# Chunk 0 of a delta-rule layer: Y from 128-row products, joint 16-blocks, and an earlier place for the second inversion

## The chip, the cores and the metric

The kernel runs on one NeuronCore of a Trainium2 chip. The metric is the device time of one execution in microseconds (us), as the median of several runs. TensorE (PE) multiplies, its weight loads (PEld) overlap with it, and VectorE (DVE), ScalarE (ACT) and GpSimd (POOL) work beside it. SyncE (SP) issues most DMAs. Each engine takes its instructions strictly in its own order and waits on semaphores of the others.

## What is computed

```python
k_n = k / (norm(k, axis=-1) + 1e-6)              # batch 4, heads 8, seq 768, head_dim 48
state = zeros(B, H, 48, 48)
for t in range(768):
    y[t] = q[t] @ state
    v_old = state^T k_n[t]
    state = state + beta[t] * outer(k_n[t], v[t] - v_old)
x = y as (3072 tokens, 384)                      # 384 = 8 heads x 48
h = x @ w_in                                     # 384 -> 2048
out = softplus(h) @ w_out                        # 2048 -> 384
```

All inputs and outputs are fp32.

## The kernel before

The sequence is cut into 12 chunks of 64 steps. In a chunk the recurrence is a triangular system: the 64x64 Gram matrix of the keys is inverted below its diagonal, and then U = T V, Y = P U and the new state follow as products. Two chunks share one inversion (`invert(u)`, u = 0 for chunks 0 and 1, u = 1 for chunks 2 and 3, ...). It works on 32x32 diagonal blocks that are spread over partitions, a row at a time, in pairs of instructions: a product into `tmp` (L294) and a sum into `Z` (L299). For u = 0 the blocks are 16x16 and two of them are done side by side, each with instructions of its own, on DVE; for later u one 32x32 block is done on POOL. Before the loop stand `norms(u)` (L222 to L242), a mask on POOL (L261) and two products on DVE (L271, L275).

The 16-blocks of chunk pair 0 are then put together by `join(s)`: a first product on PE (L324), its copy on ACT (L326), a second product on PE (L331), a subtraction and a transpose on DVE (L332, L333). `cross_a` and `cross_b` (L343) make 64x64 inverses of the 32x32 ones. `u_all` (L445) makes U, `y_all` (L476) makes Y, `state` (L457) the state.

The expert layer runs over 7 passes of 1, 1, 2, 2, ... chunks. A block of it is `hidden(i, g)` (L577, six fp32 products with 256 columns in the first pass), three ACT instructions (L582 to L584: abs, exp, ln), `softplus` on DVE (L595), and one step later `output` (L623). The weights come as 64-bit words. `feed` writes one word on an engine and starts a load, `top` makes the high halves (two casts on ACT, L525) into one of the two buffers `ex`, and `convert` puts them together on DVE (two instructions, L535) and so frees that buffer. `hidden(0, g)` needs the converted weights f = 2g and 2g + 1.

Nothing is scheduled by a planner up to the first block: the order is that in which the program is written, on every engine. Afterwards `plan` hangs steps at blocks: what stands at t is issued behind `hidden` of block t, what stands at t + 0.5 behind its `softplus` and its weight steps.

`y_all(0)` needs the layer's input as 3 tiles of 128 rows, each made of two heads' 48 rows and two 16-row pieces of a fourth pair's heads. The products have 64 rows per head, so the 16-row pieces are moved by six DMAs from x4 to x (L495), three issued by SP and three by ACT. `warm` (L684) issues products whose result nobody reads.

Of the kernel before, what the change touches and what calls it, by code (L numbers as in the profile page):

```python
# [21 lines left out]
P = 128  # L22
# [12 lines left out]
PULL0 = 8000  # L35
# [25 lines left out]
def deltanet_moe(ctx, tc, kT, qT, kI, vN, beta, wts, out, outT):  # L61
# [58 lines left out]
    GRAM_COPIES, OFFS = ((nc.scalar.copy, nc.scalar.copy),) * 2, {}  # L120

# [30 lines left out]
    tmp = const.tile([P, 2 * n_tmp], F32, name="tmp")  # L152

# [65 lines left out]
    def norms(u, lq):  # L219
# [21 lines left out]
        nc.vector.tensor_scalar(ncT, cT, -1.0, None, op0=ALU.mult)  # L241
        nc.vector.transpose(nn, nt)  # L242
        for j in range(2):
            NN[2 * u + j] = nn[:, j * NP:(j + 1) * NP]
        yield 900
        return cT, ncT

    def invert(u):
# [10 lines left out]
        for a in blocks:  # L259
            d = (slice(None), slice(a, a + n), slice(a, a + n))  # L260
            nc.gpsimd.affine_select(  # L261
                out=lq[d], in_=lq[d],
                compare_op=ALU.is_gt, fill=0.0, base=0, pattern=[[1, n], [-1, n]],
                channel_multiplier=0)
# [4 lines left out]
        for a in blocks:  # L269
            d = (slice(None), slice(a, a + n), slice(a, a + n))  # L270
            nc.vector.tensor_tensor(lq[d], lq[d],  # L271
                                    ncT[:, a:a + n].unsqueeze(1).to_broadcast([P, n, n]),
                                    op=ALU.mult)
            yield 200 + n * n
            nc.vector.tensor_tensor(Z[d], lq[d],  # L275
                                    cT[:, a:a + n].unsqueeze(2).to_broadcast([P, n, n]),
                                    op=ALU.mult)
            yield 200 + n * n
        if u < N16:

            parts = one.tile([P, 2, NP, HB + QB], F32, name=f"x{u + 1}")
            for j in range(2):
                ld = LDS[2 * u + j] = parts[:, j, :, 0:HB]
                LDS[2 * u + j, 1] = parts[:, j, :, HB:]
                nc.gpsimd.memset(ld[:, :, QB:], 0.0)
                nc.scalar.activation(ld[:, :, 0:QB], LTD[u][:, j * NP:(j + 1) * NP, 0:QB],
                                     AF.Copy, scale=half)
        engine.tensor_copy(Z.rearrange("p a b -> p (a b)")[:, 0:HB * HB:HB + 1], cT)
        for j in range(n - 2, 0, -1):
            r = n - 1 - j  # L290
            t = [tmp[:, k * n_tmp:k * n_tmp + r * j].rearrange("p (r j) -> p r j", j=j)
                 for k in range(len(blocks))]
            for a, o in zip(blocks, t):
                engine.tensor_tensor(  # L294
                    o, Z[:, a + j + 1:a + n, a + j:a + j + 1].to_broadcast([P, r, j]),
                    lq[:, a + j:a + j + 1, a:a + j].to_broadcast([P, r, j]), op=ALU.mult)
            for a, o in zip(blocks, t):
                z = Z[:, a + j + 1:a + n, a:a + j]
                engine.tensor_tensor(z, z, o, op=ALU.add)  # L299
            yield cost * 2 * len(blocks) * (160 + r * j)  # L300
# [4 lines left out]
    def turn_back(u):  # L305
        nc.vector.transpose(TT[u][:, :, HB:].rearrange("p q c -> p c q"),
                            Z.rearrange("p c j -> p j c"))
# [120 lines left out]
    def p_half(s, g):  # L428
        pt = hid([P, 8, C])
        for i in range(8):  # L430
            for ab in range(2):
                nc.tensor.matmul(pt[tk[ab], i, :], kts[s][dr[ab], 8 * g + i, :],
                                 bv[dr[ab], ab, 8 * g + i, 0:C], start=True, stop=True)
        return pt

    def mask_p(g, ab, pt):
        gs = slice(8 * g, 8 * g + 8)
        nc.vector.tensor_tensor(
            bv[tk[ab], ab, gs, 0:C], pt[tk[ab]],
# [561 lines left out]
```

## Time and profile before

| | us |
|---|---|
| median of 3 runs | 570.24 |
| lowest and highest | 569.12, 572.97 |
| span of the profiled execution | 568.9 |

Of the span PE is busy 543.8 us (96%), PEld 447.6 (79%), DVE 372.8 (66%), ACT 362.2 (64%), POOL 196.4 (35%). The mean granted TensorE clock is 0.979. The chain of work that ended last is 75% PE, 9% DVE, 7% POOL, 3% ACT, 2% DMA. The instruction stream of PE itself comes by DMA too: queue 8, kind "instruction", 60 packets, 0.98 MB. The rest is read from timelines: each row gives a start, a duration, the engine, the line of the kernel, the operation with its tiles and shapes, how many instructions were merged, and in brackets the idle time ahead of it with what ended it.

### The profile page before, as it was taken

Reading aid. Unit: us, or ns where it says so; the run is one execution under the profiler, and the core shown is the slowest. Engines: PE = TensorE matmul, PEld = TensorE weight load, DVE = VectorE, ACT = ScalarE, POOL = GpSimd, SP = SyncE. Lnnn points to the kernel's source line nnn. Section 1 sums busy time; section 2 is a strip of 40 time slices with the busy share of each in tenths; the row PEclk is TensorE's granted clock in tenths of the full one; section 3 lists DMA queues with packets and bytes.
Section 4 is the critical chain, followed back from the end, with each engine's and each line's share of the span. In section 5 each row is a group of like instructions: output and inputs, shape, how many; then the busy total and the mean of one; then the engine's idle time right before and its main releaser. Section 6 shows DMA issues by size and latency. Waiting matters only on the chain.

```text
span 568.9 us, 18018 instructions
## 1 busy us (share of the span) xinstructions
PE 543.8 (96%) x7683; PEld 447.6 (79%) x7683; DVE 372.8 (66%) x721; ACT 362.2 (64%) x702; POOL 196.4 (35%) x338
## 2 busy tenths in 40 slices
PE   4678998999999999999999999999999999999997
PEld 4456776789997888887888888888888888888885
DVE  5968785999947777548947477947375647343434
ACT  4525869898857983745873756863657855455353
POOL 4301898007982048810688000797000000000000
PEclk9857999999999999999999999999999999999999
DMA  9666862313340123220123220021220020010001
GB/s 202 169 221 206 222 208 73 72 58 72 86 99 3 31 50 79 54 69 36 31 55 73 57 71 30 3 65 35 70 86 3 1 51 22 15 57 0 1 1 55
DMA packets 35697, 39.69 MB, mean 70 GB/s; under 512 B 22625, under 2 KB 25409, under 8 KB 35617
## 3 DMA queue, kind: packets, MB, share of 16 engines
q1 hardware_dynamic: 35376, 38.23, 25.5%
q8 instruction: 60, 0.98, 0.8%
q10 hardware_dynamic: 240, 0.31, 0.2%
q14 instruction: 21, 0.16, 0.1%
HBM read 31.55 MB, written 4.72 MB: 64 GB/s over the span
## 4 chain that ended last, share of the span: by engine, by line
PE 75%; DVE 9%; POOL 7%; ACT 3%; issue 2%; DMA 2%; ACTq 0%; SPq 0%; DVEq 0%
PE po L623 30%; PE ph L577 29%; PE pa L476 4%; POOL Z L299 4%; POOL tmp L294 3%; PE pa L410 3%; PE pa L445 2%; PE pa L370 1%; PE po L684 1%; DVE big L424 1%; PE pa L457 1%; PE ph L457 1%; DMA kt<-kT 1%; DVE a L589 1%; DVE tt L303 1%
## 5 line engine op out<-in xcount | busy, mean ns | idle before, releaser
L577 PE MATMUL ph<-x,b 128*128 128x512 f32 (+1 forms) x576 | 166.2, 373 | 0.0
L582 ACT ACTIVATE a<-ph 128x512 f32<-128x512 f32 x96 | 57.4, 598 | 149.2 <-PE ph L577 146.6
L577 PE MATMUL ph<-x,a 128*128 128x512 f32 (+1 forms) x384 | 130.8, 378 | 1.8 <-DMA x<-x 1.8
L589 DVE SCALAR_TENSOR_TENSOR a<-ph,a 128x512 f32<-128x512 f32 x88 | 60.4, 686 | 93.2 <-ACT a L584 92.6
L577 PEld LDWEIGHTS ph<-x,b 128*128 128x128 f32 x576 | 105.1, 188 | 19.3
L623 PE MATMUL po<-gh,b 128*128 128x512 f32 (+1 forms) x241 | 97.6, 405 | 1.4 <-DVE gh L591 1.4
L623 PE MATMUL po<-gh,a 128*128 128x512 f32 (+1 forms) x241 | 94.0, 390 | 0.0
L299 POOL TENSOR_TENSOR Z<-Z,tmp 128x30 f32<-128x30 f32 (+9 forms) x150 | 89.4, 596 | 11.8
L294 POOL TENSOR_TENSOR tmp<-Z,ltq 128x30 f32<-128x30 f32 (+9 forms) x150 | 85.7, 571 | 11.4
L577 PEld LDWEIGHTS ph<-x,a 128*128 128x128 f32 x384 | 73.2, 191 | 15.6 <-issue 2.2
L592 DVE TENSOR_TENSOR gl<-a,gh 128x512 fp32r<-128x512 f32 x88 | 66.2, 752 | 7.8 <-DVE gh L591 0.5
L623 PE MATMUL po<-gl,b 128*128 128x512 f32 (+1 forms) x241 | 69.3, 388 | 0.0
L584 ACT ACTIVATE a<-a 128x512 f32<-128x512 f32 x96 | 60.7, 632 | 3.1
L583 ACT ACTIVATE a<-a 128x512 f32<-128x512 f32 x96 | 60.6, 632 | 3.0
L623 PEld LDWEIGHTS po<-gh,b 128*128 128x128 f32 x241 | 45.2, 187 | 12.7 <-DVE gh L591 1.9
L623 PEld LDWEIGHTS po<-gl,b 128*128 128x128 f32 x241 | 45.2, 188 | 9.6
L623 PEld LDWEIGHTS po<-gh,a 128*128 128x128 f32 x241 | 45.3, 188 | 8.5
L261 POOL TENSOR_SCALAR_AFFINE_SELECT ltq<-ltq 128x1024 f32<-128x1024 f32 (+1 forms) x7 | 8.4, 1203 | 115.7 <-DVE ss L222 115.7
L591 DVE CAST gh<-a 128x512 fp32r<-128x512 f32 x88 | 41.3, 470 | 7.8 <-DVE a L589 0.5
L484 DVE TENSOR_TENSOR x<-pa,x 128x384 fp32r<-128x384 f32 x20 | 11.1, 555 | 39.9 <-ACT x L482 39.9
L623 PE MATMUL po<-a,gh 128*128 128x384 f32 x96 | 33.5, 445 | 0.0
L476 PEld LDWEIGHTS pa<-big 128*64 128x64 f32 x704 | 23.5, 143 | 7.3 <-issue 4.3
(160 smaller groups left out, 746.7 us busy)
## 6 DMA issues: line engine op xcount, KB each, us to landing
a<-wts SPq DMA_DIRECT2D x16, 383.8 KB, 3.7
b<-wts SPq DMA_DIRECT2D x16, 383.8 KB, 4.5
kt<-kT SPq DMA_DIRECT2D x24, 192.0 KB, 3.5
big<-qT SPq DMA_DIRECT2D x24, 192.0 KB, 4.1
nv<-vN SPq DMA_DIRECT2D x12, 384.0 KB, 3.4
ki<-kI SPq DMA_DIRECT2D x24, 192.0 KB, 3.3
outT<-ot SPq DMA_DIRECT2D x13, 256.0 KB, 2.3
x<-x SPq DMA_DIRECT2D x66, 32.0 KB, 2.0
```

What stands on the lines that cost most here:

```text
L294: engine.tensor_tensor(o, Z[:, a + j + 1:a + n, a + j:a + j + 1].to_broadcast([P, r, j]), lq[:, a + j:a + j + 1, a:a + j].to_broadcast([P, ...
L299: engine.tensor_tensor(z, z, o, op=ALU.add)
L410: nc.tensor.matmul(pks[e][tk[t], i % 4, :], kt[dr[ab], p, :], bv[dr[ab], ab, p, :], start=True, stop=True)
L476: nc.tensor.matmul(py[tk[ab], i, :], big[:, at + C:at + 2 * C], big[:, at:at + C], start=True, stop=True)
L577: nc.tensor.matmul(ph[:, j], weight(i, f, a, k * P, P), xr[b][k], start=(c == 0), stop=(c == len(terms) * NK - 1))
L582: nc.scalar.activation(a, ph, AF.Abs)
L583: nc.scalar.activation(a, a, AF.Exp, scale=-1.0)
L584: nc.scalar.activation(a, a, AF.Ln, bias=1.0)
L589: nc.vector.scalar_tensor_tensor(a, ph, 0.0, a, op0=ALU.max, op1=ALU.add)
L591: nc.vector.tensor_copy(hi_lo[0], a)
L592: nc.vector.tensor_tensor(hi_lo[1], a, hi_lo[0], op=ALU.subtract)
L623: nc.tensor.matmul(PO[i][h][:, c], l, r, start=(fs[j] == 0 and m == 0), stop=(fs[j] == NF - 1 and m == k - 1 and c != (cut and parts[0])))
```

## The change

The change rewrites the work on chunk 0 up to the first blocks of the expert layer.

- **Y of chunk 0.** `first_p`, `first_u` and `first_y` place U and P so that one product with 128 rows of contraction gives a 128-row tile of the layer's input, with the 16-row pieces in place. U goes to a zeroed tile `still`. The six DMAs and the tile x4 are gone. There are 48 products for P (32 before), 32 for U (32), 24 for Y (32). `rest_of_u` copies a part of U to `big` on POOL, since `first_state` still needs it.
- **Joint 16-blocks.** `diagonal` gives both 16-blocks as one access pattern: the two products before the loop, and each step's product and sum, are one instruction each, of twice the elements. The mask on POOL is one instruction over the whole tile.
- **Second inversion.** Its first transpose (L280 of the new file, L255 before) stands on DVE ahead of the end of the first join, its norms around U and Y. `first_state` and the first product of `join(1)` stand behind `hidden(0, 0)`, the rest of `join(1)` behind the first softplus.
- **Smaller ones.** `turn_back` transposes 16 columns instead of 32. Some of the one-word writes of `feed` go to ACT. The three converts that stood together ahead of the second norms are spread. `warm` reads a constant tile, in other banks. Three memsets are added at the start.

```diff
+    def diagonal(t, blocks, n, r0, c0, nr, nc_, wide=(True, True)):
+        dims = [t.ap[0]] + ([(n * (HB + 1), len(blocks))] if len(blocks) > 1 else [])
+        dims += [(HB if wide[0] else 0, nr), (1 if wide[1] else 0, nc_)]
+        return bass.AP(t.tensor, t.offset + r0 * HB + c0, dims)
...
-            for a, o in zip(blocks, t):
-                engine.tensor_tensor(
-                    o, Z[:, a + j + 1:a + n, a + j:a + j + 1].to_broadcast([P, r, j]),
-                    lq[:, a + j:a + j + 1, a:a + j].to_broadcast([P, r, j]), op=ALU.mult)
-            for a, o in zip(blocks, t):
-                z = Z[:, a + j + 1:a + n, a:a + j]
-                engine.tensor_tensor(z, z, o, op=ALU.add)
+            engine.tensor_tensor(o, diagonal(Z, blocks, n, j + 1, j, r, j, (True, False)),
+                                 diagonal(lq, blocks, n, j, 0, r, j, (False, True)),
+                                 op=ALU.mult)
+            z = diagonal(Z, blocks, n, j + 1, 0, r, j)
+            engine.tensor_tensor(z, z, o, op=ALU.add)
...
+    def first_p(g):
+        pts = [first_banks[2 * g + ab]() for ab in range(2)]
+        for b in range(2):
+            for t in range(NK):
+                for ab in range(2):
+                    for h, p in ((ab, 8 * g + 4 * b + t), (1 - ab, 8 * g + 4 * b + NK)):
+                        nc.tensor.matmul(pts[ab][tk[h], NK * b + t, :], kts[0][dr[ab], p, :],
+                                         bv[dr[ab], ab, p, 0:C], start=True, stop=True)
+        return pts
...
+    def first_y():
+        X[0] = one.tile([P, NK, 1, 1, B, C], F32, name="x0")
+        for g in range(2):
+            py = bank([P, 2 * NK, C])
+            for b in range(2):
+                for t in range(NK):
+                    for ab in range(2):
+                        nc.tensor.matmul(py[tk[ab], NK * b + t, :], still[:, ab, 2 * g + b, t, :],
+                                         bv[:, ab, 8 * g + 4 * b + t, 0:C], start=True, stop=True)
+            copies[g](X[0][:, :, 0, 0, 2 * g:2 * g + 2, :],
+                      py.rearrange("p (b t) c -> p t b c", t=NK))
+        load_q(1)
...
-        turn_back(0)
-        feed()
-        turn(0, 0, QB)
-        mask_p(0, 0, pts[0])
-        feed()
-        mask_p(0, 1, pts[0])
-        mask_p(1, 0, pts[1])
+        turn_back(0, QB)
+        turn(0, 0, QB)
+        feed(1, nc.scalar.copy)
+        convert()
+        top()
+        feed(1, nc.scalar.copy)
+        iv = invert(1)
+        next(iv)
         run(jn)
         warm(512)
-        feed(2)
+        feed(1, nc.scalar.copy)
         arrange(0, 1)
+        for k in range(3):
+            first_mask(k // 2, k % 2)
         cross_a(0)
...
-        u_all(0)
+        next(iv)
+        first_u()
+        rest_of_u()
         warm(512)
-        feed(2)
-        background.append([invert(1), 7700, 8])
-        pull(1)
-        y_all(0)
+        feed(1, nc.scalar.copy)
+        convert()
+        first_y()
         load_v(1)
-        pull(1)
-        convert()
-        feed()
+        for _ in range(4):
+            next(iv)
+        run(iv)
+        feed(2)
         top()
         convert()
-        feed()
+        feed(2)
+        top()
+        convert()
         top()
         jn = join(1)
-        state(0)
-        load_ki(1)
-        next(jn)
-        convert()
-        top()
-        pull(PULL0)
...
-        at(0, 1200, bind(run, jn))
+        at(0, 1200, first_state, bind(next, jn))
+        at(0.5, 0, bind(run, jn))
```

How this stands in the engines' orders, at three places. In the rows `L...` is the line of the file in question, behind it the operation, the tile written, the tiles read, the shape of what is written, and how many follow each other.

PE, from the products of Y of chunk 0 to the second block's `hidden`, before (L476 is Y, L457 the state, L324 and L331 the two products of `join(1)`, L577 `hidden`):

```order
L476 MATMUL pa<-big 64x64 x32
L457 MATMUL pa<-big,ki 48x48 x16
L457 MATMUL po_855<-big,ki 48x48 x16
L324 MATMUL pa<-tt,x_284 32x16 x64
L577 MATMUL ph_1020<-x_762,a_94 128x256 x3
L577 MATMUL ph_1020<-x_762,a_298 128x256 x3
L331 MATMUL pa<-x_284,tt 32x16 x64
L577 MATMUL ph_1117<-x_762,a_328 128x256 x3
```

The same place now (L508 is Y, L521 the state, L340 and L347 the two products of `join(1)`, L659 `hidden`):

```order
L508 MATMUL pa<-big,ot 64x64 x12
L659 MATMUL ph_894<-x_765,a_96 128x256 x3
L659 MATMUL ph_894<-x_765,a_315 128x256 x3
L521 MATMUL pa<-ot,ki 48x48 x6
...
L340 MATMUL po_945<-tt,x_217 32x16 x64
L347 MATMUL pa<-x_217,tt 32x16 x64
L659 MATMUL ph_1097<-x_765,a_333 128x256 x3
```

The first block now stands ahead of the state and of both products of `join(1)`, and nothing stands between these two any more.

DVE, from the last copy of Y on, before (L535 are the converts of three weights, two rows each; L231 to L275 the second norms and the two products):

```order
L482 COPY x_762<-pa 128x3x128
L222 COPY ss<-ltq 128x32
L227 TENSOR_SCALAR rt<-ss 128x32
L535 SCALAR_TENSOR_TENSOR a_298<-a_298,ex 128x384
L535 SCALAR_TENSOR_TENSOR a_298<-b_313,ex 128x384
...
L535 SCALAR_TENSOR_TENSOR a_358<-b_457,ex 128x384
L231 RECIPROCAL r_815<-rt 128x32
...
L271 TENSOR_TENSOR ltq<-ltq,ncT 128x1024
L275 TENSOR_TENSOR Z<-ltq,cT 128x1024
L332 TENSOR_TENSOR tt<-tt,pa 128x16x16
```

The same place now (L617 are converts):

```order
L510 COPY x_765<-pa 128x3x128
L244 RECIPROCAL r_704<-rt 128x32
...
L299 TENSOR_TENSOR ltq<-ltq,ncT 128x1024
L301 TENSOR_TENSOR Z<-ltq,cT 128x1024
L595 COPY b_872<-half 128x1
L595 COPY a_875<-half 128x1
L617 SCALAR_TENSOR_TENSOR a_333<-a_333,ex 128x384
L617 SCALAR_TENSOR_TENSOR a_333<-b_342,ex 128x384
...
L617 SCALAR_TENSOR_TENSOR a_443<-b_516,ex 128x384
L677 SCALAR_TENSOR_TENSOR gh<-ph_894,a 128x512
```

The converts of the third and fourth weight (a_333, a_443) stood ahead of the second norms and products, and stand behind them now.

ACT, from the copy of Y to the first block's abs, before (L495 are the row moves, L525 casts of `top`, L460 copies of the state, L326 the copy between the two products of `join(1)`):

```order
L482 COPY x_762<-pa 128x3x128
L495 DMA x_762<-x_763 16x256 x3
...
L525 CAST ex<-a_531 128x384
L525 CAST ex<-b_536 128x384
L460 COPY big<-pa 48x8x48 x2
L460 COPY big<-po_855 48x8x48 x2
L326 COPY x_284<-pa 128x16x16
L525 CAST ex<-a_610 128x384
L525 CAST ex<-b_613 128x384
L582 ACTIVATE a<-ph_1020 128x512
```

The same place now (L607 are casts of `top`, L664 to L666 the first block's abs, exp, ln, L524 copies of the state, L342 the copy between the two products of `join(1)`):

```order
L510 COPY x_765<-po_766 128x3x128
...
L607 CAST ex<-a_523 128x384
L607 CAST ex<-b_597 128x384
L607 CAST ex<-a_643 128x384
L607 CAST ex<-b_646 128x384
L664 ACTIVATE a<-ph_894 128x512
L665 ACTIVATE a<-a 128x512
L666 ACTIVATE a<-a 128x512
L524 COPY big<-pa 48x8x48 x4
L342 COPY x_217<-po_945 128x16x16
```

The copy between the two products of `join(1)` stood ahead of the first block's abs, and stands behind it now, with the state's copies between.

## Rows read from the trace of the kernel before

**Rows 1.** Busy time by stretch: us, each engine's busy time (instructions), granted clock, DMA.

```profile
54.15:58.77 4.62, 4.59 (x137) 3.72 (x137) 3.48 (x8) 3.50 (x8) 0.74 (x4) 0.68 1.01 311
58.77:568.90 510.13, 501.72 (x6504) 415.51 (x6503) 330.15 (x582) 336.02 (x640) 181.54 (x306) 1.00 0.21 54
29.90:46.80 16.90, 14.37 (x350) 9.64 (x351) 10.43 (x24) 3.87 (x10) 1.04 (x2) 0.50 0.71 228
53.80:57.00 3.20, 2.82 (x7) 2.31 (x8) 2.99 (x9) 2.72 (x7) 0.00 (x0) 0.50 1.00 297
```

**Rows 2.** The chain that ended last, where the first block begins: start, us, what.

```profile
50.18 3.87 DMA x<-x
...
58.77 2.79 PE ph L577 x12
```

**Rows 3.** Timeline of DVE, first inversion: start, us, line, operation, count.

```profile
10.50 2.07 DVE L255 STREAM_TRANSPOSE ltq<-work 128x1024 f32<-128x1024 f32 x1
...
13.56 0.65 DVE L535 SCALAR_TENSOR_TENSOR a<-b,ex 128x384 int32<-128x384 int32 x1
...
16.30 0.98 DVE L271 TENSOR_TENSOR ltq<-ltq,ncT 128x256 f32<-128x256 f32 x1
...
18.11 1.02 DVE L275 TENSOR_TENSOR Z<-ltq,cT 128x256 f32<-128x256 f32 x1
...
25.86 0.29 DVE L299 TENSOR_TENSOR Z<-Z,tmp 128x14 f32<-128x14 f32 x2
...
26.18 1.04 DVE L303 STREAM_TRANSPOSE tt<-Z 128x512 f32<-128x512 f32 x1
...
27.09 1.94 DVE L306 STREAM_TRANSPOSE tt<-Z 128x1024 f32<-128x1024 f32 x1
...
34.14 0.42 DVE L332 TENSOR_TENSOR tt<-tt,pa 128x256 f32<-128x256 f32 x1 [1.91 <-PE pa L331]
...
37.13 0.88 DVE L355 TENSOR_SCALAR off<-po 32x256 f32<-32x256 f32 x2 [1.73 <-PE pa L343]
```

**Rows 4.** DVE by line and shape, 19.2 to 26.2 us: count, busy us, mean ns.

```profile
L294 DVE TENSOR_TENSOR tmp<-Z,ltq 128x56 f32<-128x56 f32 x4 | 0.7, 208 | 0.0
...
L294 DVE TENSOR_TENSOR tmp<-Z,ltq 128x14 f32<-128x14 f32 x4 | 0.5, 172 | 0.0
```

**Rows 5.** Timeline of PE ahead of the first block.

```profile
12.01 3.54 PE L432 MATMUL ph<-big,kt 48*64 48x64 f32 x61 [0.73 <-DMA big<-qT]
...
27.36 1.25 PE L324 MATMUL pa<-tt,x 32*32 32x16 f32 x128 [2.39 <-DVE b L513]
...
32.38 1.68 PE L331 MATMUL pa<-x,tt 32*32 32x16 f32 x110 [2.85 <-issue]
...
40.32 0.35 PE L445 MATMUL pa<-nv,tt 64*64 64x48 f32 x2
...
42.70 2.07 PE L684 MATMUL po<-a 128*128 128x512 f32 x2
44.70 3.05 PE L476 MATMUL pa<-big 128*64 128x64 f32 x64
...
54.18 3.40 PE L577 MATMUL ph<-x,a 128*128 128x256 f32 x8 [1.84 <-DMA x<-x]
```

**Rows 6.** Timeline of DVE, second inversion's start and the first converts behind it.

```profile
53.15 0.35 DVE L231 RECIPROCAL r<-rt 128x32 f32<-128x32 f32 x1
...
56.58 1.23 DVE L275 TENSOR_TENSOR Z<-ltq,cT 128x1024 f32<-128x1024 f32 x1
...
60.61 0.55 DVE L535 SCALAR_TENSOR_TENSOR a<-a,ex 128x384 int32<-128x384 int32 x1
```

**Rows 7.** Timeline of ACT: state copies, the join's copy, and the second block's ln.

```profile
53.35 0.96 ACT L460 COPY big<-pa 48x384 f32<-48x384 f32 x2
...
55.17 0.36 ACT L326 COPY x<-pa 128x256 f32<-128x256 f32 x1
...
65.03 0.63 ACT L584 ACTIVATE a<-a 128x512 f32<-128x512 f32 x1
```

## What I expect, and why

> **What bounds the kernel now.** I read the busy time by stretch first. From 58.77 us to the end PE is busy 501.72 of 510.13 us at the full clock [rows 1]. So the expert layer runs on PE, and whatever stands ahead counts only by when PE gets there. The chain of waits then shows how the layer begins: PE waits for the row moves, whose last DMA is under way from 50.18 to 54.05 us, and the second block starts at 58.77 [rows 2]. I take the second block's start as the mark, because by then PE has done the same work in both programs: Y, the state, `join(1)` and the first block. The sum asks where this mark comes to lie. From the timelines the reader is to see who paces the stretch ahead of it: DVE until the first transposes [rows 3], PE at half clock from 29.9 to 46.8 us [rows 1, 5], then the DMA.
>
> **The first inversion.** Four edits on DVE. (a) The converts leave the norms. Their second half runs from 13.56 to 14.21 us [rows 3] while the norms could go on: up to 0.6 us gained. (b) Four products of 256 elements take from 16.30 to 19.13 us, 2.83 us [rows 3]. Two of 512 elements replace them; 256 take 0.42 us (L332) [rows 3] and 1024 take 1.23 [rows 6], so 512 take 0.7: 1.4 gained. (c) The norms' transpose goes behind the loop: 0.1. (d) The loop runs from 19.2 to 26.15, 6.9 us. Now it has 28 instructions instead of 56, each of twice the elements. One of 14 elements takes 172 ns, one of 56 takes 208 [rows 4], a slope of 0.86 ns for an element. But two of 14 end within 0.29 us [rows 3]: the two blocks' instructions overlap, and a step takes as long as product and sum of one block, one behind the other. The joint ones can't overlap, since each sum reads the product ahead of it. With 28 to 112 elements they take 184 to 256 ns, and some 30 ns lie between dependent ones: 28 x 0.26 = 7.3 us. So the loop loses 0.4. Bounds: a loss of 1.2 where the wider pattern costs as much per element as the 1024-element product (1.2 ns), and a gain of 3.4 where halving the instructions halves the loop. I take the loss of 0.4, as the rows have the overlap. Sum: 1.7 us earlier, the end at 24.5.
>
> The Trainium skill, page "VectorE: DVE Perf Modes", section "The TRN2 errata", says that each instruction on SBUF operands pays a fixed latency between instructions, so many small ones pay it each and a large one once. By that rule the loop would take about half, 3.5 us, and the inversion would end at 20.7; the row of two instructions in 0.29 us speaks against it here.
>
> **The first join.** DVE goes on with the first transpose (1.04), half of the second (1.94 before, so 1.0) and the third (1.04): until 27.6. The first weight's converts (twice 0.6) and the second inversion's transpose (2.07) are put ahead of the join's subtraction [rows 3, 6]: DVE is ready for it at 30.9. On PE the first product can start at 25.6 and takes 1.25; copy 0.4; the second product 1.25 to 1.95 (110 take 1.68 at half clock) [rows 5]: until 29.2 at the latest, if nothing stops it. But before, PE stood still for 2.85 us in that product, and waited for nothing that the profile shows ("issue") [rows 5]. Weights were arriving all the while, and PE's own instructions come by DMA, so I take it for late instructions. The same number of instructions into the program now falls near the end of the join's first product, and the next such place near the end of the second. So the subtraction starts between 30.9 (gap covered by DVE) and 32.1 (gap in full). I take 31.9: 2.2 earlier than 34.14.
>
> **To the first block.** From the subtraction to U it took 34.14 to 40.32, 6.2 us [rows 3, 5], at half clock, with the same useless products between; the three masks of P (384 elements each, 0.55 by the two prices above) fit into the 1.73 us that DVE waits ahead of L355 [rows 3]. U starts at 38.1. Its order uses two corners of the array at a time in three of four products, where 61 products of P with 64 columns took 3.54 us in such an order [rows 5], which gives 2.8 for 64 of 48 columns; before it took 2.4 (40.32 to 42.70). I take 2.6. The useless products behind it take 2.07; Y has 48 matmuls where 64 took 3.05: 2.3; the copy of Y, 384 elements, takes 0.55 like another of that shape [rows 5, 6]. POOL's copy of U is needed only by the state, some 4 us later. The first block can start at 38.1 + 2.6 + 2.1 + 2.3 + 0.6 = 45.7, with no row moves, against 54.18 for the bulk of it before: **8.5 us earlier**.
>
> **To the second block.** This is where the forecast is decided. `join(1)`'s second product stands in PE's order ahead of the second block, and needs ACT's copy L342. In ACT's order that copy stands behind the state's copies, these behind the first block's abs, exp and ln, and these behind the casts of two weights, which need buffers that DVE's converts free. Those converts now stand behind the second norms and products. So:
> - DVE from the end of Y's copy at 45.7: norms and products 4.7 (53.15 to 57.81) [rows 6], until 50.4.
> - From the start of a first convert to the end of ln of the block behind it: 5.05 us (60.61 to 65.66, two converts, four casts, abs, exp, ln, all back to back) [rows 6, 7]. Same chain here: until 55.5.
> - The state's four copies and the join's copy: 2.2 (53.35 to 55.53) [rows 7]: until 57.7.
> - PE's second product: 1.25 to 1.95 [rows 5]: the second block starts at 59.0 to 59.7.
>
> Before it was 58.77. So of 8.5 us gained nothing is left: **+0.2 to +0.9, I take +0.5**. PE itself would be done much sooner: first block (12 matmuls, 425 ns each at half clock, 216 at full [rows 2, 5]) by 49, state 1.5, join's first product 1.25: it stands from about 51.5 to 57.8.
>
> **The clock.** Before, a wait of 1.84 us ahead of 54.18 [rows 5] was followed by a stretch at clock 0.50 [rows 1]. A wait of 6 us will do no less. The second block then starts at half clock, where 12 matmuls take 5.1 us instead of 2.6: 0 to +2.5, I take **+1.5**, as before it took 3 us of dense work (54.18 to 57.1) to come back. Part of this comes back later: DVE and ACT work on while PE is slow, and PE's 8.4 idle us behind 58.77 [rows 1] hold some waits for them. 0 to 2 us, I take **-0.7**.
>
> **The sum.** 0.5 + 1.5 - 0.7 = +1.3 us. The profiled 568.9 become 570.2. The median of the runs lies 1.34 above the span: 570.24 + 1.3 = **571.5**. One per cent, 5.7 us, is about what a measurement of this kernel can tell from no change, so "same" reaches from 564.5 to 575.9.
>
> **Rivals.**
> - *The gain holds* (0.10). PE finds the join's copy in time, because DVE or ACT do the converts or casts earlier than I read. Then from 45.7: first block 3.3, state 1.5, products 1.25 + 1.25: the second block at 53.0, 5.8 earlier, no clock lost: 570.24 - 5.8 = 564.4. Against it: the orders above, which the engines can't change.
> - *Slower* (0.10). The wait of PE takes the clock down for longer than one block. What decides is whether the granted clock is still 0.50 when the third block starts. Before, it stayed at 0.50 for 16.9 us although PE was busy for 14.37 of them [rows 1], so coming back isn't certain. Two more blocks of 6 us at half clock would lose 6 in place of 1.5: 576.0.
> - *The prologue is as late as before* (0.05). U and Y go as slowly as P's first products, or instruction gaps come twice (2.85 more): Y's copy at 48.5, all behind it 2.8 later: 574.3.
> - *The loop halves* (0.05). By the rule cited, as a mechanism: two instructions of one shape cost one. 3.8 us off the loop against my sum, of which DVE passes 2.5 on, as the gap on PE stays: 569.0.
> - *The wait is there, the clock isn't* (0.15, within the main case's range): +0.5 - 0.7: 570.0.
>
> **Chances.** The likeliest is the forecast itself, gain eaten by the wait for the join's copy and some clock (0.55): 571.5, between 569.0 and 574.0. Faster by over 1% is the first rival: 0.10. Slower by over 1%: the second rival: 0.10. Within 1%: 0.80. The range has to leave out 2 in 10 at most, so it takes in the third, fourth and fifth rival and ends short of the first and at the edge of the second: 567.0 to 575.5.
>
> **What would show it.** In the profile of the changed kernel: the loop L309/L313 as long as before or a little longer; the first block's matmuls (L659) starting near 46; PE idle for some 6 us ahead of L347, with ACT's L342 as releaser; L664 starting only near 53.5, right behind casts that waited for L617; clock 0.50 where the second block starts; from the third block on the same rhythm as before. Wrong, if L664 starts right behind the first block's matmuls, if the gap ahead of L347 is under 2 us, or if PE has its full clock before 40 us: each would bring the mark 2 to 6 us forward.

## The result, and the profile after

| | before | changed |
|---|---|---|
| median of 8 runs, us | 570.7 | 574.31 |
| lowest and highest, us | 568.14, 572.97 | 569.47, 577.18 |
| span of the profiled execution, us | 568.9 | 567.7 |

The ratio to the kernel before is 1.0057, with a 95% interval of 1.0032 to 1.0083. So the change costs about half a per cent. The profiled execution is the quickest of the eight, and 1.2 us shorter than that of before; the other seven have spans up to 7.8 us longer. Both facts have to be explained. In the profiled executions of e0 and e5 and in one execution of e6 below, TensorE was slow throughout (2963.9, 2366.2 and 770.53 us), and all medians and ratios leave them out.

First the profiled execution. Busy time by stretch of the changed kernel (as in [rows 1]: length, busy time and instructions of PE, PEld, DVE, ACT and POOL, granted clock, DMA share, GB/s):

```profile
44.60:58.12 13.52, 7.42 (x332) 6.64 (x332) 10.24 (x27) 8.23 (x17) 7.82 (x16) 0.87 0.91 258
58.12:567.70 509.58, 502.91 (x6511) 416.31 (x6503) 326.50 (x575) 333.14 (x635) 174.65 (x294) 1.00 0.20 54
...
54.50:61.30 6.80, 5.01 (x136) 4.34 (x137) 4.34 (x10) 3.82 (x9) 6.01 (x11) 0.50 1.00 296
```

The second block starts at 58.12 us and the rest takes 509.58 us. Before, the same kind of view, a timeline of PE, has the second block at 58.70 (the chain in [rows 2] has 58.77), and the rest took 510.20:

```profile
58.70 2.86 PE L577 MATMUL ph<-x,a 128*128 128x256 f32 x12
```

The first block, however, starts at 44.60, 9.6 us ahead of the bulk of it before [rows 5]. Of the 13.5 us between the two starts PE works 7.4. Its timeline shows where the rest went:

```profile
25.90 1.25 PE L340 MATMUL pa<-tt,x 32*32 32x16 f32 x128 [0.92 <-DVE a L595]
...
27.71 1.14 PE L347 MATMUL po<-x,tt 32*32 32x16 f32 x114
32.07 0.40 PE L347 MATMUL po<-x,tt 32*32 32x16 f32 x14 [3.22 <-issue]
...
44.60 2.83 PE L659 MATMUL ph<-x,a 128*128 128x256 f32 x12 [0.73 <-ACT ex L607]
...
48.93 1.26 PE L340 MATMUL po<-tt,x 32*32 32x16 f32 x128
56.29 1.90 PE L347 MATMUL pa<-x,tt 32*32 32x16 f32 x128 [6.10 <-ACT x L342]
58.12 4.41 PE L659 MATMUL ph<-x,a 128*128 128x256 f32 x12
```

PE has the state and `join(1)`'s first product done at 50.2 and waits 6.10 us for ACT's copy L342. The second block then takes 4.41 us where it took 2.86, as the granted clock has fallen to 0.50 (row 54.50 above). What held the copy is in ACT's timeline, and behind it in DVE's:

```profile
49.70 0.63 ACT L607 CAST ex<-a 128x384 f16<-128x384 bf16 x1 [5.01 <-DVE a L617]
...
52.11 0.59 ACT L664 ACTIVATE a<-ph 128x512 f32<-128x512 f32 x1
...
54.05 1.93 ACT L524 COPY big<-pa 48x384 f32<-48x384 f32 x4
55.88 0.36 ACT L342 COPY x<-po 128x256 f32<-128x256 f32 x1
```

```profile
16.94 0.18 DVE L309 TENSOR_TENSOR tmp<-Z,ltq 128x28 f32<-128x28 f32 x1
...
24.47 0.21 DVE L313 TENSOR_TENSOR Z<-Z,tmp 128x28 f32<-128x28 f32 x1
...
32.56 0.42 DVE L348 TENSOR_TENSOR tt<-tt,po 128x256 f32<-128x256 f32 x1 [2.03 <-PE po L347]
...
44.42 0.34 DVE L244 RECIPROCAL r<-rt 128x32 f32<-128x32 f32 x1
...
49.11 0.55 DVE L617 SCALAR_TENSOR_TENSOR a<-a,ex 128x384 int32<-128x384 int32 x1
```

ACT stands 5.01 us ahead of its cast, for a convert that DVE reaches at 49.11, after the second norms and products. From there ACT works without a gap to the end of L342. This is the chain of the forecast. At the other end of the listing stands the 3.22 us in L347, a gap in which PE waits for nothing that the profile shows; the experiments come back to it.

### The profile page after: what moved, and what is told of

Its sections match the earlier page's. It is cut to its first block, busy times and chain, and to the rows that moved or that the text cites. A ratio compares the mean times of both kernels' runs of the same rounds, so it can differ in the third digit from the quotient of the medians.

```text
span 567.7 us, 18023 instructions
## 1 busy us (share of the span) xinstructions
PE 541.4 (95%) x7699; PEld 445.9 (79%) x7699; DVE 370.5 (65%) x687; ACT 363.3 (64%) x712; POOL 196.9 (35%) x339
## 4 chain that ended last, share of the span: by engine, by line
PE 70%; DVE 12%; POOL 7%; ACT 5%; issue 3%; DMA 2%; SPq 0%; ACTq 0%; DVEq 0%
PE po L705 28%; PE ph L659 27%; POOL Z L313 4%; POOL tmp L309 3%; PE pa L561 3%; PE pa L426 2%; PE pa L386 2%; DVE big L440 1%; PE pa L530 1%; PE pa L542 1%; DVE a L617 1%; PE ph L542 1%; PE pa L769 1%; DMA a<-wts 1%; ACT ex L607 1%
## 5 line engine op out<-in xcount | busy, mean ns | idle before, releaser
L659 PE MATMUL ph<-x,b 128*128 128x512 f32 (+1 forms) x576 | 166.2, 373 | 0.0
L664 ACT ACTIVATE a<-ph 128x512 f32<-128x512 f32 x96 | 57.4, 598 | 152.5 <-PE ph L659 149.9
L659 PE MATMUL ph<-x,a 128*128 128x512 f32 (+1 forms) x384 | 130.7, 378 | 0.7 <-ACT ex L607 0.7
L659 PEld LDWEIGHTS ph<-x,b 128*128 128x128 f32 x576 | 105.1, 188 | 19.3
L659 PEld LDWEIGHTS ph<-x,a 128*128 128x128 f32 x384 | 73.4, 192 | 14.4 <-ACT ex L607 0.8
L666 ACT ACTIVATE a<-a 128x512 f32<-128x512 f32 x96 | 60.7, 632 | 3.0
L286 POOL TENSOR_SCALAR_AFFINE_SELECT ltq<-ltq 128x1024 f32<-128x1024 f32 x6 | 7.6, 1268 | 109.5 <-DVE ss L235 109.5
L440 DVE TENSOR_TENSOR big<-pa,maskP 64x256 f32<-64x256 f32 x66 | 27.8, 421 | 1.0
```

Of the source, the lines that this page charges most:

```text
L440: nc.vector.tensor_tensor(be[tk[ab], ab, e, 4 * g:4 * g + 4, 0:C], pks[e][t, :, 0:C], maskP[t].unsqueeze(1).to_broadcast([C, 4, C]), op=AL ...
L659: nc.tensor.matmul(ph[:, j], weight(i, f, a, k * P, P), xr[b][k], start=(c == 0), stop=(c == len(terms) * NK - 1))
L664: nc.scalar.activation(a, ph, AF.Abs)
L666: nc.scalar.activation(a, a, AF.Ln, bias=1.0)
```

## Experiments

In the tables below "mark" is the start of the second block, "stop" a gap on PE that the profile puts down to "issue". Ratios are to the kernel before.

**The changed kernel once more.** No edit.

> The changed kernel once more, unedited, for a second profiled execution and more runs. The first profiled execution took 567.7 us at a mean clock of 0.984 and was the quickest of its eight; the others had spans up to 575.5 at clocks of 0.969 to 0.981. Theory: the order of events up to 58 us is the same each time (first block's matmuls at 44.6, wait for L342 of 6.1 us, second block at 58.1), and a slower execution differs by more stretches at clock 0.50 ahead of or behind that wait: for each stretch of about 3.4 us of dense work at 0.50, 1.7 us. Ratio to the kernel before 1.003 to 1.008. Rival: slower executions begin the first block later (a load that comes late): then the first block's start moves by as much as the time.

Median 573.92, ratio 1.0058 [1.0033, 1.0084], as at first. Its profile can't be used, so the question what makes an execution long stays open here.

> The changed kernel, unedited, once more with a profile, since the first repetition was disturbed. Theory (the median of the changed kernel lies 3 to 5 us above its first profile because in most executions PE stops for instructions twice in the first join, at its instruction 961 and again at 1217, where the first profile shows only the second): either the first profile comes again (567.5 to 569 us, first block at 44 to 45, one stop of 3 us), or an execution of 571 to 575 us with two stops, together 4 to 6 us, first block at 48 to 50 and the same wait of 6.1 us ahead of L347 behind it. Rival (slower executions differ by a late load or by the clock alone): 571 to 575 us with one stop and the first block at 44 to 45.5.

A single execution of 571.13 us, span 569.4. It has one stop in the first join, and the first block at 44.98. Its order of events is that of the first profile, but by its time it fits the words of the rival (571 to 575 us with one stop). Of the 1.7 us that it is longer than the first profile, 0.4 lie ahead of the mark and 1.3 behind it, so a stop in the first join isn't all that makes an execution long:

```profile
31.83 0.41 PE L347 MATMUL po<-x,tt 32*32 32x16 f32 x14 [2.67 <-issue]
...
56.67 1.90 PE L347 MATMUL pa<-x,tt 32*32 32x16 f32 x128 [6.09 <-ACT x L342]
58.50 4.79 PE L659 MATMUL ph<-x,a 128*128 128x256 f32 x12
```

**The kernel before once more.** No edit.

> The kernel before, unedited, once more with a profile. Theory: one stop for instructions in the first join (at 961, 2.9 us in its first profile), none at 1217, since that place lies among its larger products; second block at 57 to 60. Rival: two stops here too, second block beyond 61; then the stops don't tell the two kernels apart.

A single execution of 572.48 us, span 570.8, mark at 59.56. One stop again, 2.98 us in the first join's second product, where [rows 5] has 2.85. Here too the second block runs at half clock, 4.58 us. So in both pairs of profiles with one stop the changed kernel has the shorter span, by 1.2 and 1.4 us.

```profile
32.35 1.68 PE L331 MATMUL pa<-x,tt 32*32 32x16 f32 x110 [2.98 <-issue]
...
59.56 4.58 PE L577 MATMUL ph<-x,a 128*128 128x256 f32 x12
```

**The joint loop undone.**

```diff
-            engine.tensor_tensor(o, diagonal(Z, ...), diagonal(lq, ...), op=ALU.mult)
-            engine.tensor_tensor(z, z, o, op=ALU.add)
+            for a, o in zip(blocks, t):
+                engine.tensor_tensor(o, Z[...a...], lq[...a...], op=ALU.mult)
+            for a, o in zip(blocks, t):
+                engine.tensor_tensor(z, z, o, op=ALU.add)   # z of block a
```

> The loop of the first inversion alone is undone: each step's product and sum are again two instructions each, of 16-blocks side by side (56 in place of 28, every second one overlapping). Everything else as in the changed kernel. Theory (two small instructions overlap, one joint one costs what the longer of the pair's chain costs): the loop, 16.9 to 24.7 us in the changed kernel with four one-word writes in it (7.7 us), takes about 7.3, that is 6.9 as in the kernel before and 0.4 for the writes. Rival (halving the instructions nearly halves the loop): it takes 11 to 14 us.

DVE's first and last row of the loop, and then PE's rows around the first join and the second block (from the sums on, line numbers are one higher in this file):

```profile
17.32 0.25 DVE L309 TENSOR_TENSOR tmp<-Z,ltq 128x14 f32<-128x14 f32 x2
...
24.51 0.27 DVE L314 TENSOR_TENSOR Z<-Z,tmp 128x14 f32<-128x14 f32 x2
```

```profile
26.22 1.16 PE L341 MATMUL pa<-tt,x 32*32 32x16 f32 x117
30.20 0.40 PE L341 MATMUL pa<-tt,x 32*32 32x16 f32 x11 [2.82 <-issue]
...
31.67 1.78 PE L348 MATMUL po<-x,tt 32*32 32x16 f32 x114
34.47 0.40 PE L348 MATMUL po<-x,tt 32*32 32x16 f32 x14 [1.02 <-issue]
...
48.32 2.83 PE L660 MATMUL ph<-x,a 128*128 128x256 f32 x12 [0.74 <-ACT ex L608]
...
60.01 1.90 PE L348 MATMUL pa<-x,tt 32*32 32x16 f32 x128 [6.10 <-ACT x L343]
61.84 5.20 PE L660 MATMUL ph<-x,a 128*128 128x256 f32 x12
```

56 instructions take 17.32 to 24.78, 7.46 us; the 28 joint ones took 16.94 to 24.68, 7.74. So the joint form loses 0.3 us, with the same four one-word writes inside. The Trainium skill, page "VectorE: DVE Perf Modes", section "The TRN2 errata", says that many small instructions pay a latency each and one large one pays it once; by that rule half as many instructions would take about half the time, an estimate. The 7.46 and 7.74 us don't agree with it here.

The same 56 instructions took 6.9 us in the kernel before (the forecast's own reading, 19.2 to 26.15). So 0.6 us of what the loop is longer by aren't due to the joint form; no run shows what they are due to.

The execution shows something more: two stops in the first join, after 117 recorded matmuls (two for each product) of the first and after 114 of the second, a first block at 48.32 and the mark at 61.84. Its span is 572.2, of which 510.4 lie behind the mark, as in the others with this order (509.6 to 511.2). Against the first profile the first block is 3.7 us later: 2.4 by the join's subtraction (34.96 against 32.56), the rest mostly by the clock, which is at 0.50 until 46.1 us here and came back at 40.8 there.

**DVE's order.** The converts of weights 3 and 4 ahead of the second norms and products.

```diff
+        feed(2); top(); convert(); feed(2); top(); convert(); top()
         for _ in range(4):
             next(iv)
         run(iv)
-        feed(2); top(); convert(); feed(2); top(); convert(); top()
         jn = join(1)
```

> On DVE the converts of weights 3 and 4 (with their one-word writes) stand ahead of the second norms and products instead of behind them; PE, ACT and POOL keep their order. Theory (the wait for L342 is the converts' place on DVE): converts at 44.5 to 46.8 instead of 49.1 to 51.6; the casts follow, L664 at about 47.7 instead of 52.1, L342 done at about 51.8 instead of 56.2, PE's wait ahead of L347 1.7 us instead of 6.1, second block at about 53.1 instead of 58.1, and at full clock: 6 us less than the changed kernel, ratio to the kernel before 0.993 to 0.998. Rival (the casts wait for their loads, not for DVE): L664 stays near 52, ratio 1.004 to 1.008. Second rival (gain given back later, since POOL's second inversion starts 2.4 us later): second block at 53, but a new wait of PE behind it, ratio 1.003 or more.

Median 571.24, ratio 1.0016 [0.9995, 1.0038]: half of what was expected. The wait moved as the theory has it: ACT's L664 starts at 47.15 (52.11 before the edit) and L342 ends at 51.3. But PE, in the profiled execution (span 567.7):

```profile
51.34 0.55 PE L347 MATMUL pa<-x,tt 32*32 32x16 f32 x42 [1.31 <-ACT x L342]
55.22 1.36 PE L347 MATMUL pa<-x,tt 32*32 32x16 f32 x86 [3.33 <-issue]
56.51 5.17 PE L659 MATMUL ph<-x,a 128*128 128x256 f32 x12
```

Of 6.1 us of waiting 1.31 are left, and a stop of 3.33 stands in the middle of the product. In the changed kernel the same place lay behind the 6.1 us. So the mark is 1.6 us earlier, not 5, and the clock falls all the same: PE idles 4.6 of 5.2 us. The span, 567.7, is that of the changed kernel's first profile: the 1.6 us are gone again behind the mark, half of them in the second block (5.17 against 4.41). So what shortens the median by some 3 us isn't seen in this pair of profiles.

**PE's order.** The second product of `join(1)` behind the first block's output.

```diff
-        at(0.5, 0, bind(run, jn))
-        at(1, 0, bind(cross_a, 1), bind(arrange, 1, 1))
-        at(2, 920, bind(cross_b, 1), bind(scale_v, 1))
+        at(1.5, 0, bind(run, jn))
+        at(2, 0, bind(cross_a, 1), bind(arrange, 1, 1))
+        at(2.5, 920, bind(cross_b, 1), bind(scale_v, 1))
```

> The second product of join(1) (L347) stands behind the first block's output in PE's order instead of ahead of the second block; cross_a and cross_b of chunk 1 stand half a step later; DVE and ACT keep their order up to the second block. Theory (only the place of L347 holds the second block back): second block at 51.7, when the converts of weights 3 and 4 are done, instead of 58.1; PE waits 1.5 us there instead of 6.1, the clock stays at 1.0; the join's product of 1.3 us comes later. So 5 us plus 1.6 of clock less than the changed kernel, ratio to the kernel before 0.993 to 0.998. Rival (PE is held by what is behind the state and join on ACT anyway): it then waits as long for the first softplus or for L347 behind it, ratio 1.002 to 1.008.

Median 572.81, ratio 1.0041 [1.0022, 1.0059]. The profiled execution (span 573.2) has two stops in the first join (3.34 and 1.69) and its first block at 50.02, 5.4 us later than the first profile, though nothing ahead of that block was edited. Behind it the second block follows without a wait and at full clock, as expected; but what was put behind it is now late:

```profile
55.54 2.86 PE L659 MATMUL ph<-x,a 128*128 128x256 f32 x12
60.21 2.85 PE L705 MATMUL po<-a,gh 128*128 128x384 f32 x8 [1.82 <-DVE b L595]
...
70.20 1.07 PE L359 MATMUL pa<-tt,off 32*32 32x32 f32 x64 [3.17 <-DVE tt L348]
```

The subtraction L348 now stands behind the second softplus and two more weights' converts on DVE, and `cross_a` waits 3.17 us for it: the rival in part, a wait that was moved.

**Both.** DVE's order of e1, and the second product directly behind the second block (`at(1, ...)`, `cross_a` at 1.5).

> Converts of weights 3 and 4 ahead of the second norms on DVE (as in e1_converts_first), and the second product of join(1) directly behind the second block in PE's order, cross_a of chunk 1 behind the first block's output. Theory (two things held the second block back: the wait for L342, and behind it PE's own instructions, which come late wherever 512 of them run through in 3 us): the second block starts right behind the join's first product, at 50.2 us in an execution whose first join has one stop for instructions, L347 behind it needs no wait for L342, and the second block's 2.8 us give PE's instructions time to arrive. Mark 50 to 51 against 56.5 in e1_converts_first and 58.1 in the changed kernel; with 1.3 us of join moved behind it and the full clock, 5 to 6 us less than e1_converts_first: 565 to 567, ratio to the kernel before 0.989 to 0.994. Rival (the engines behind it, ACT above all, cannot follow, and PE waits later): ratio 0.998 to 1.002.

Median 570.90, ratio 1.0014 [0.9990, 1.0037]: no better than e1 alone. It has no profile that can be used, so where the gain went is read from two kernels that hold the same edits (below).

**PE kept busy in its wait.**

```diff
+        def busy():
+            pw = lent([P, 512])
+            for _ in range(10):
+                nc.tensor.matmul(pw, even[:, 0:P], even, start=True, stop=True)
...
-        at(0, 1200, first_state, bind(next, jn))
+        at(0, 1200, first_state, bind(next, jn), busy)
```

> Ten products of 512 columns that nobody reads stand between the first and the second product of join(1), in PE's wait (about 5.6 us of the 6.1 at full clock). Nothing else is moved. Theory (the clock falls because PE stands still there, and costs what the second block shows): L347 still at about 56.2, but 1.3 us long instead of 1.9, and the second block 2.8 us instead of 4.4: 2.2 us less than the changed kernel, and the spread of its runs smaller; ratio to the kernel before 1.000 to 1.004. Rival (the half clock there costs nothing, since DVE and ACT work on and PE waits for them later): same time as the changed kernel, 1.004 to 1.008. Second rival (the products delay L347): 1.008 or more.

Median 576.26, ratio 1.0106 [1.0071, 1.0141]: slower. The ten products take 8.85 us, not 5.6 (I had read the price of one product, which is recorded as two instructions, as that of two), so they delay L347. The second rival came in, and the total says nothing on the clock. One row does:

```profile
53.48 8.85 PE L939 MATMUL ph<-gl 128*128 128x512 f32 x20
62.26 1.26 PE L347 MATMUL pa<-x,tt 32*32 32x16 f32 x128
63.45 2.86 PE L659 MATMUL ph<-x,a 128*128 128x256 f32 x12
```

With PE busy through the wait the granted clock is 1.00 from the first block to the end of the second, which takes 2.86 us instead of 4.41 to 5.20 (changed kernel, e10, e4), and L347 takes 1.26 instead of 1.90. So PE's idle time takes the clock down, and this costs 2.2 to 3.0 us at that place. This execution too has two stops in the first join (3.62, 2.11).

**The place in PE's stream.** 57 products that nobody reads stand ahead of the third Gram product, 228 instructions.

```diff
         systems(1)
+        for k in range(4):
+            pw = bank([P, 512])
+            for _ in range(15 if k == 3 else 14):
+                nc.tensor.matmul(pw[0:HB, 0:QB], even[0:HB, 0:HB], even[0:HB, 0:QB],
+                                 start=True, stop=True)
         gram(2)
```

> 57 products of 16 columns that nobody reads, 228 instructions of PE, stand ahead of the third Gram product, where PE waits about 2 us for its keys; nothing else is changed. In all traces so far PE stops with no wait at its instruction 961 or 1217 (counted in the records), and later at 2241 or 2497, which are 256 apart; in the changed kernel 961 lies in the first join's first product (L340) and 1217 near the end of its second (L347). Theory (instructions are fetched in blocks of 256, and PE stops where a block is late): the stops move 228 instructions back in the program, to the very start of L347 and to just behind it, so there is at most one stop inside the first join, none within 110 products of L347's end, and the join's subtraction comes at 30.6 to 33; in join(1) the stop lies in L347's wait or products. The first block starts at or ahead of 44.6, and the median falls by 2 to 4 us from the changed kernel's: ratio to the kernel before 0.999 to 1.003. Rival (the stops belong to these products, their banks or their weights, not to the place in the stream): they stay after 117 products of L340 and 114 of L347, ratio 1.004 to 1.008.

Median 574.83, ratio 1.0081 [1.0051, 1.0111]. The products on one corner of the array took 6.3 us, not the 2 us of PE's wait, so all behind them is later and the time is no test. The place of the stop is one:

```profile
31.62 1.24 PE L347 MATMUL po<-x,tt 32*32 32x16 f32 x127
35.29 0.20 PE L347 MATMUL po<-x,tt 32*32 32x16 f32 x1 [2.43 <-issue]
```

The stop after 117 matmuls of L340 doesn't occur in this execution, and the one in L347 stands after 127 instead of 114. The expected place was one matmul further on, just behind L347. It is at instruction 1473, counted over all records that PE has in the trace (matmuls, weight loads, and its waits), that is 256 behind 1217. So the stop belongs to the place in the stream, not to these products.

**The same with cheap products.** 56 products, on four corners in turn.

> As e6_shift_fetch, but 56 products on four corners of the array in turn (1.1 us, as 64 of L340 take 1.25) instead of 57 on one corner, which took 6.2 us and made PE later. 224 instructions: PE's instruction 1473 is then just behind the end of L347 of the first join, 1217 at its start. Nothing else of the changed kernel is changed. Theory (a stop costs nothing where PE has to wait for DVE anyway): L347 ends at about 29 to 29.5 in one piece, the subtraction starts when DVE comes, at 30.5 to 31, the first block at 42.5 to 43.5 in nearly all executions, and the wait for L342 behind it stays 6.1 us: median 2 to 5 us below the changed kernel's, ratio to the kernel before 0.997 to 1.002. Rival (another stop takes its place): ratio 1.004 to 1.008.

Median 573.77, ratio 1.0074 [1.0051, 1.0098]: the rival. L347 runs through in one piece and the stop stands behind it, as expected, but another comes at instruction 705, which is 256 ahead of 961, in the third Gram product:

```profile
19.86 1.77 PE L176 MATMUL pa<-kt 48*64 48x64 f32 x56 [3.07 <-issue]
...
31.76 1.26 PE L347 MATMUL po<-x,tt 32*32 32x16 f32 x128
...
35.43 0.70 PE L769 MATMUL pa<-gl 128*128 128x512 f32 x1 [1.78 <-issue]
...
48.70 2.83 PE L659 MATMUL ph<-x,a 128*128 128x256 f32 x12 [0.74 <-ACT ex L607]
```

**With both orders as well.** e6 and e8 each joined with the edits of e5.

> e5_both_moved and e6_shift_fetch together. Theory (both price separate places, ahead of the first block and behind it): the gains add, 2 to 4 us of e6 to those of e5: 562 to 565, ratio to the kernel before 0.985 to 0.991. Rival (the stops only move on into the state and join(1)): no better than e5_both_moved.

> e8_shift_only together with e5_both_moved (converts ahead of the second norms, the second product of join(1) behind the second block). Theory: the gains of both add, second block at 48 to 50 us, no wait for L342: 563 to 567 us, ratio to the kernel before 0.985 to 0.993, faster than both kernels. Rival (behind the second block ACT and the instructions of join(1) hold PE as before): ratio 0.997 to 1.002.

Medians 571.63 and 572.14, ratios 1.0031 [1.0011, 1.0051] and 1.0036 [1.0019, 1.0053], far from the 0.985 to 0.993 expected, e9 above its rival's range too. No version is faster than the kernel before; only e1 and e5 can't be told from it. In both the second block starts 5.7 to 6.5 us behind the first, at full clock, where the changed kernel needs 13.5. What follows takes the gain back; e9:

```profile
53.96 2.86 PE L659 MATMUL ph<-x,a 128*128 128x256 f32 x12
...
59.37 0.89 PE L347 MATMUL pa<-x,tt 32*32 32x16 f32 x84 [2.07 <-issue]
...
66.12 0.44 PE L359 MATMUL pa<-tt,off 32*32 32x32 f32 x28 [2.62 <-issue]
```

Stops of 2.07 and 2.62 us in the next small products, and the first block is late (48.28), as in e8. For e5 itself this is carried over from its two relatives, not seen.

**One stop or two.** In the six profiles (without e0 and e5) in which PE's stream up to the first block is that of the changed kernel, the first join has one stop three times and two stops three times:

| execution | stops in the first join, us | first block | second block | span |
|---|---|---|---|---|
| changed kernel | 3.22 | 44.60 | 58.12 | 567.7 |
| e10, unedited | 2.67 | 44.98 | 58.50 | 569.4 |
| e1 | 2.40 | 44.28 | 56.51 | 567.7 |
| e4 | 2.82 + 1.02 | 48.32 | 61.84 | 572.2 |
| e2 | 3.34 + 1.69 | 50.02 | 55.54 | 573.2 |
| e3 | 3.62 + 2.11 | 47.96 | 63.45 | 574.6 |

What a stop waits for can be read from the transfers of the queue that carries PE's instructions (packets, MB, share of 16 engines). Within the stop of 3.22 us in the changed kernel (28.86 to 32.07), and within that of 3.33 us in e1 (51.89 to 55.22), there is one:

```profile
q8 instruction: 1, 0.02, 1.8%
q8 instruction: 1, 0.02, 1.9%
```

The first is under way from 29.85 to 30.78 us, and PE goes on at 32.07; the second from 52.53 to 53.55, and PE goes on at 55.22. The twelve profiles without e0 and e5 have 25 gaps of 0.7 us or more that are put down to "issue", and in each PE goes on 0.9 to 1.7 us after the end of such a packet. So PE stands still until a block of its own instructions has come.

The executions with one and with two stops differ in when a block comes. The same queue from 19.5 to 27 us, in the changed kernel:

```profile
q8 instruction: 1, 0.02, 0.8%
```

The one-stop executions all have this row there, the two-stop ones and both profiles of the kernel before have none. So where a block of instructions comes while PE is at the useless products ahead of the join, there is no stop at 961; this goes together in all eight, and was not forced by an edit. The packet that comes late takes no longer than the early one (0.9 to 1.1 us); it starts 5 to 7 us later.

## Why the prediction came out as it did

The forecast was 571.5 us, "same", in 567.0 to 575.5. The median came to 574.31, the ratio to 1.0057. The mechanism is right: next to nothing is left of the earlier first block, for the wait that was named. The sum is not: the profiled execution came out 2.5 us below what was worked out for it (567.7 against 570.2) and the median 2.8 above the forecast. The change was put at +1.3 us; it is -1.2 between the first profiles and +3.6 between the medians. That the median still lies within the range is owed to the range's width. The two misses have different causes.

- **First inversion.** Forecast end 24.5, measured 24.68, but by two errors that nearly cancel. The loop starts at 16.94 instead of 17.2, and it is 0.8 us longer than before instead of 0.4 (7.74 against 6.9). Of these 0.8 the joint form has 0.3 (e4); the rest stays open. The rival that the loop halves is out.
- **First join.** The subtraction was put at 31.9, one stop in full. It came at 32.04 to 32.56 in the three executions with one stop and at 34.96 to 36.88 in the three with two. **This is the term that was too small for the median**, as far as the profiles show it: "instruction gaps come twice" shared a rival with a chance of 0.05, at 574.3 us, and it holds in half of the six profiles. I had even named both places, near the end of the first and of the second product, and then priced one. That its 574.3 is the measured median to the digit is luck: e4 has its first block 2.6 us behind the forecast's 45.7, but the rest of its sum differs.
- **To the first block.** Subtraction to U 6.17 us (forecast 6.2), U 2.54 (2.6). The useless products and Y took 1.12 and 1.62 instead of 2.1 and 2.3, as the clock came back at 40.8 us, not after 46.8 as before [rows 1]. So the first block came at 44.60 instead of 45.7.
- **To the second block.** Norms and products 4.66 us (4.7), first convert to ln 4.91 (5.05), state and join copies 2.19 (2.2), L347 1.90 (1.25 to 1.95), PE's wait 6.10 ("some 6"). All terms held; the mark came at 58.12 instead of 59.0 to 59.7, for the clock of the step ahead. e1 shows by moving the converts that their place on DVE was the cause of this wait: of 6.1 us 1.31 stayed.
- **The clock.** Forecast a loss of 1.5; the second block took 1.55 more than before, and e3 shows that it is PE's idling that does it. (The 2.6 us that the forecast gives for twelve matmuls at full clock are not in [rows 2], which has 2.79.) But the kernel before pays it too in some executions (4.58 us in its second profile), so the term is no clean difference.
- **Given back later.** Forecast 0.7. In the first pair of profiles it is 2.2: the stretch behind the mark is 0.62 shorter although the second block, with which it begins, is 1.55 longer. Most of this is in PE's waits for ACT's copies near 95 us (in all, how often, the longest), before and changed:

```profile
PE pa L476 <- ACT big L449: 1.9, 4, 1.4
PE po L561 <- ACT big L534: 0.2, 1, 0.2
```

  In the second pair (510.9 against 511.2, second blocks of 4.79 and 4.58) it is 0.5. So for the first pair the forecast's three terms measure -0.6 + 1.55 - 2.2 = -1.2, where they were put at 0.5 + 1.5 - 0.7.

The sum for the median: in e4, which differs from the changed kernel only by 0.3 us on DVE, the mark is at 61.84 and the stretch behind it 510.4. That more than half of the executions of the changed kernel look like this one is inferred, not shown: of the 20 on record, nine have spans of 567.7 to 571.1 us and eleven of 572.2 to 575.9; e4's is 572.2, but the changed kernel's own two profiles, 567.7 and 569.4, were both of the other kind. What makes the longest still longer, by up to 3.7 us, no profile shows. The slow rival (half clock beyond the second block) did not occur in its profiles: the third block takes 2.75 us in both, as at full clock.

The rival "the gain holds" (564.4) failed twice over. The wait for L342 was there; and with it gone, e1, e7 and e9 show the next thing that PE lacks, its own instructions. Why a block comes early in one execution and late in the next stays open.

## What to carry to other kernels

Pulling a stage forward pays only as far as the engines behind it have their inputs: before you move work ahead, follow the order of every engine to the next product that can't be moved, here PE to ACT's copy, ACT to its casts, casts to DVE's converts. A gap that the profile puts down to "issue" is a cost of its own, and it may hide under a wait: whoever takes the wait away meets it. Look then at the queue of kind "instruction" in the same stretch. One profiled execution is one draw; where two kinds of execution exist, compare spans over the runs with the profile's before making a sum from it.

## What the runs showed of the hardware

- **PE's stops for instructions lie on a grid.** Counted over all records of PE (matmuls, weight loads, waits), the stops of 0.7 us or more come at 705, 961, 1217, 1473, 1729, 2241, 2497 and 2753, all multiples of 256 apart, whatever product stands there, and last 0.8 to 3.6 us. The instruction queue moves 0.98 MB in 60 packets, 16 KB each, for 15,538 such records: about 64 bytes a record, 256 records a packet. The kernels with useless products added, 15,578 to 15,768 records, have 61 packets.
- **Speed alone doesn't make a stop.** PE had run through the 256 records ahead of a stop in 1.2 to 6.4 us; other stretches of 256 that took 1.2 to 2.0 us pass without one, such as the first join's first product and what stands around it in e6 (1.28 us).
- **Small products cost by the corners they use.** 84 recorded matmuls of 16 columns (two for each product) on one corner of the array take 4.66 us (e6), 82 on four corners in turn 1.41 (e8), both at a granted clock of 1.00.
